# Reciprocal deviations regrouped by a small TensorE product instead of a trip through DRAM, and the third batch entry's spectrum and way back moved to later steps

## The chip, the core and the metric

One Trainium2 chip, one of its cores. The metric is the device time of one execution in microseconds (us), given as the median of several runs. Beside the runs there is one profiled execution, with a trace of every instruction; its own time and its span stand in the table below. All data are 32-bit floats.

## What is computed

The reference is a global filter over the sequence followed by a feed-forward block with a SoLU activation and a layer norm:

```python
X = np.fft.rfft(x, axis=1)                 # x: 8 entries x 3136 positions x 256 channels
Y = X * (filt_r + 1j * filt_i)[None]
x = np.fft.irfft(Y, n=3136, axis=1).reshape(25088, 256)

h = x @ w_in                               # 256 -> 1024
e = np.exp(h - max(h)); sm = e / (sum(e) + 1e-9)
solu = h * sm
ln = (solu - mean(solu)) / np.sqrt(var(solu) + 1e-6) * g_ln
out = ln @ w_out                           # 1024 -> 256
```

Maxima, sums, means and variances are taken over the 1024 features of each of the 25088 tokens. The factor 1 / sqrt(var + 1e-6) is one number per token. In the kernel it is called rs, and it is applied at the very end, when a token's output leaves PSUM.

## The kernel before, in words

**The feed-forward half** sets the rhythm. The 25088 tokens are 196 blocks of 128; two blocks make a pair, two pairs a group of four blocks (so 98 pairs and 49 groups). The program is an order written out by hand under a manual schedule: `step(k)` is called for k = 0 to 204, and each step issues work for several blocks at different ages. With j = k // 2, an even step and the odd step after it make the seven products of a 2 x 2 Strassen-like scheme for pair j (`product`, L723, on sums and differences that `pair_sums` makes on GpSimd), and the seven products of the output side for an older pair p (`project`, L844; p = j - 5 in the even step, j - 4 in the odd one). Each engine runs its own instructions in the order in which the program issues them.

Each `product` is one matmul of 128 x 512, each `project` four matmuls of 128 x 128; the trace shows every such float matmul as two weight loads and two matmul records. The results of a `project` stand in two PSUM banks, o0 and o1. ScalarE takes one out, scaled by rs (`keep_out`, L856), VectorE adds the other, scaled by rs too (`finish_out`, L860).

Between the two halves of a pair: exponential (ScalarE, L755), normalization (VectorE, L771), the sum of squares (`square`, ScalarE, L779, which leaves the variance), a transpose of 32 x 32 squares (`turn`, VectorE, L787), and the regrouping of the transposed squares by eight DMAs on SP's queue (`regroup`, L799). GpSimd then makes the sums of the output side (`project_sums`, L702).

**The deviations.** The variances of a group lie as [128 partitions, 4 blocks]. After the regrouping, the tokens stand on other partitions: row 32 b + i of a new block a holds what was row 32 a + i of old block b. So rs has to be regrouped in the same way. The kernel before does that through DRAM, once per group: in the even step, `deviations` makes rs on GpSimd (L806 and L808) and writes it by one DMA on SP's queue (L810, 2 KB); in the odd step after it, `regroup_deviations` reads it back by four DMAs on SP's queue (L816, 0.5 KB each, in pieces of one number). Only for the last group these five DMAs are on GpSimd's queue. `keep_out` and `finish_out` of the group's first pair follow some two steps later.

**The filter half** is a Fourier transform in stages, for entries 0 to 7. Entry 0 is transformed up front; each later entry is woven into the steps by the table `PLAN`, which gives three lists of steps per entry: its first stage (eight pieces), its spectrum (seven pieces) and its way back (eight pieces). For entries 2 to 7 a first-stage piece fetches a slice of x (SP's queue, L245), forms a difference on VectorE (L254) and a sum on GpSimd (`sum`, L260), multiplies late in step t (L269), and stores its result to DRAM in step t + 1 (GpSimd's queue, L280). A spectrum piece in step t fetches its part of all eight first-stage results (`fetch`, L291) and its tables (`fetch_de`, L683) on ScalarE's queue and its filter on GpSimd's queue (L642), multiplies in step t (L301), multiplies by the filter on VectorE (L322 to L324), transforms back in step t + 1 and stores in step t + 2. These fetches stand in the list `spectrum_loads[t - 2]`, which runs in the middle of step t - 2; for entry 1's pieces before step 8 and for the first piece of entry 2 they stand at the end of step t - 2 instead, in `loads`. A piece of the way back (`fetch_back` on GpSimd's queue, L356; `back_halves`, L372; `join_halves`, L385 and L386) writes 4 x 2 of the positions into `y`, from which the tokens are read. Where two pieces of the way back share a step, the second is put at the step's end.

Entry 2's spectrum stands at steps 16, 18, ..., 28 and its way back at steps 32, 34, ..., 46; its eight first-stage pieces at 5, 7, 8, ..., 13. Entry 1's way back is at steps 16 to 22.

Of the kernel before, what the change touches and what calls it, by code (L numbers as in the profile page):

```python
# [9 lines left out]
FP32 = mybir.dt.float32  # L10
I32 = mybir.dt.int32
AFT = mybir.ActivationFunctionType
ALU = mybir.AluOpType
AX = mybir.AxisListType
PSUM = bass.MemoryType.PSUM
DRAM = bass.MemoryType.DRAM

P = 128
B, S, C = 8, 3136, 256
DFF = 1024  # L20
# [16 lines left out]
PLAN = [  # L37
    None,
    ([0, 0, 0, 0, 1, 1, 1, 1], [4, 5, 6, 7, 8, 10, 12], [16, 17, 18, 19, 20, 20, 21, 22]),
    ([5, 7, 8, 9, 10, 11, 12, 13], range(16, 30, 2), range(32, 48, 2)),  # L40
    ([15, 23, 25, 27, 29, 31, 33, 35], range(38, 52, 2), range(54, 70, 2)),
    (range(39, 55, 2), range(58, 72, 2), range(76, 92, 2)),
    (range(63, 79, 2), range(82, 96, 2), range(100, 116, 2)),
# [3 lines left out]
EPS_LN, EPS_SM = 1e-6, 1e-9  # L47
# [47 lines left out]
def kernel(  # L95
# [10 lines left out]
    nc = tc.nc  # L106
# [3 lines left out]
    wi_dram = nc.inline_tensor(wi_host, name="wi_tbl").ap()  # L110
    wb_dram = nc.inline_tensor(wb_host, name="wb_tbl").ap()
    de_dram = nc.inline_tensor(de_host, name="de_tbl").ap()

    def pool(name, bufs, space=None, stack=ctx):
        kw = {} if space is None else {"space": space}
        return stack.enter_context(tc.tile_pool(name=name, bufs=bufs, **kw))
# [4 lines left out]
    small = pool("sm", 4)  # L121
# [14 lines left out]
    neg_half = consts.tile([P, 4], FP32, name="neg_half")  # L136
# [265 lines left out]
    with ExitStack() as st:  # L402
# [50 lines left out]
        second = Spectrum(1, None, None, None)  # L453
# [136 lines left out]
        for i0, n, rows in ((0, 4, P), (4, 4, P), (8, NP - 9, P), (NP - 1, 1, NQ)):  # L590
            f, at = filters[i0]
# [19 lines left out]
    def psum(name):  # L611
        return ps_t.tile([P, 2, C], FP32, name=name, tag="t")

    def psum_pair(name, other):
# [7 lines left out]
    hpool = pool("hp", 2)  # L622
    wk = pool("wk", 1)
    spool = pool("sp", 1)
    rs_dram = pool("rs_dram", 2, DRAM)
    pools |= {name: pool(name + "1", bufs)
             for name, bufs in (("r", 4), ("diff", 1), ("t2", 1), ("p", 1), ("g", 1))}
    pools["de"] = pool("de1", 2)
    second.pools = pools
    for c, at, n, kind, dims in (  # L630
            (0, 0, 4 * C, "t2", "p (v c) -> p v c"), (0, 4 * C, 4 * C, "f", "p (v k c) -> p v k c"),
# [48 lines left out]
    def load_de(sp, u):  # L680
# [3 lines left out]
                            in_=de_dram[i:i + pairs].rearrange("i p k u q -> p i (k u q)"))  # L684
        return de

    turns, variances, solu_ts, solu_sums, rs_rows, rss, pos, ots = (
        {} for _ in range(8))
    sums, ms, hs, nmaxs, es, solus, squares = {}, {}, {}, {}, {}, {}, {}


# [107 lines left out]
            nc.sync.dma_start(out=st[32 * q:32 * q + 32, :, :],  # L799
                              in_=turned[32 * a:32 * a + 32, :, q, :])  # L800

    def deviations(p, dma):
        g, second = divmod(p, 2)
        if not second:
            rs = small.tile([P, 4], FP32, name=f"rs_{g}", tag="rs", bufs=2)
            nc.gpsimd.tensor_scalar(out=rs, in0=variances.pop(g), scalar1=1.0 / DFF, scalar2=EPS_LN,  # L806
                                    op0=ALU.mult, op1=ALU.add)
            nc.gpsimd.tensor_tensor(out=rs, in0=rs, in1=neg_half, op=ALU.pow)  # L808
            rs_rows[g] = rows = rs_dram.tile([P, 4], FP32, name=f"rows_{g}", tag="rows")
            dma(out=rows, in_=rs)  # L810

    def regroup_deviations(g, dma):
        rows = rs_rows.pop(g).rearrange("(a p) b -> b p a", p=32)
        rss[g] = small.tile([P, 4], FP32, name=f"rs_t_{g}", tag="rs_t")
        for b in range(4):
            dma(out=rss[g][32 * b:32 * b + 32, :], in_=rows[b])  # L816

    def project_sums(p, step):

# [14 lines left out]
    def project(p, m):  # L834

        bank = {1: 0, 6: 0, 5: 0, 3: 0, 2: 1, 7: 1, 4: 1}[m]
        if m in (1, 2):
            pos[p, bank] = ps_o.tile([P, DFF // 2], FP32, name=f"o{m}_{p}", tag=f"o{bank}")[:, 0:P]
        s1, s2, s3, s4 = solu_sums[p]
        lhs = {1: solu_ts[p, 0][0], 2: solu_ts[p, 0][1], 4: solu_ts[p, 1][1], 5: s1, 6: s2, 7: s3,  # L840
               3: s4}[m]
        w = w_out_sb[:, {1: 0, 2: 1, 3: 2, 5: 3, 6: 4, 7: 5, 4: 6}[m]]
        for f in range(KF // 2):
            nc.tensor.matmul(out=pos[p, bank], lhsT=lhs[:, f, :], rhs=w[:, f, :],  # L844
                             start=f == 0 and m in (1, 2, 7), stop=True, skip_group_check=True)
# [32 lines left out]
    def ahead(t, by):  # L878
        return loads[max(0, t - by)]
# [3 lines left out]
    for e in range(1, B):  # L883
        first_at, spectrum_at, back_at = PLAN[e]
        sp = Spectrum(e, pools, load_filter, load_de)
        if e == 1:
            sp = second
            sp.load, sp.load_de = load_filter, load_de
        for i, t in enumerate(first_at):
            dma = nc.gpsimd.dma_start  # L890
            if e == 1:
                if i not in sp.xs:
                    row_loads.append((t, t - 1, -1, lambda sp=sp, i=i, dma=dma: sp.fetch_x(i, [dma] * 2)))
                for u in range(2):
                    (early, late)[u][t].append(lambda sp=sp, i=i, u=u: sp.first(
                        i, (u,), psum(f"pa_{sp.e}_{i}_{u}").rearrange("p a c -> p (a c)").rearrange(
                            "p (o n) -> p o n", o=1), nc.scalar.copy, sp.xs[i][0:NK, 2 * u:2 * u + 2, :]))
                    (early, late)[u][t].append(lambda sp=sp, i=i, u=u: sp.store_first(
                        i, 2 * u, nc.gpsimd.dma_start))
            else:  # L900

                row_loads.append((t, t - 2, -1, lambda sp=sp, i=i: sp.fetch_quarters(i, nc.sync.dma_start)))
                stores[t].append(lambda sp=sp, i=i: sp.difference(i))
                products[t].append(lambda sp=sp, i=i: sp.sum(i))
                late[t].append(lambda sp=sp, i=i: sp.first_quarters(
                    i, [psum(f"pa_{sp.e}_{i}_{g}") for g in range(2)]))
                stores[t + 1].append(lambda sp=sp, i=i, dma=dma: sp.store_quarters(i, dma))
        for i, t in enumerate(spectrum_at):

            other = e == 1 and i % 2 == 1 and t + 1 < LAG  # L910


            dma = nc.sync.dma_start if e == 1 and t < 8 else nc.scalar.dma_start
            fetches = ahead(t, 2) if e == 1 and t < 8 or e == 2 and i == 0 else spectrum_loads[t - 2]
            fetches.append(lambda sp=sp, i=i, dma=dma: sp.fetch(i, dma))
            ahead(t, 1 if e == 1 and i % 2 == 1 else 2).append(lambda sp=sp, i=i: sp.fetch_filter(i))
            fetches.append(lambda sp=sp, i=i: sp.fetch_de(i))
            early[t].append(lambda sp=sp, i=i, o=other: sp.forward(i, psum_pair(f"pb_{sp.e}_{i}", o)))
            add = (nc.gpsimd if t + 1 < LAG else nc.vector).tensor_tensor
            first_parts[t].append(lambda sp=sp, i=i, add=add: sp.multiply(i, 0, add))  # L920
            (top if t + 1 < LAG else second_parts)[t + 1].append(
                lambda sp=sp, i=i, add=add: sp.multiply(i, 1, add))
            late[t + 1].append(lambda sp=sp, i=i, o=other: sp.inverse(i, psum_pair(f"pc_{sp.e}_{i}", o)))
            stores[t + 2].append(lambda sp=sp, i=i: sp.store(i, nc.gpsimd.dma_start))


        assert S * (e - 1) <= P * (back_at[0] // 2 * 2) and P * (back_at[-1] + 2) <= S * e // P // 2 * 2 * P
        for ch, t in enumerate(back_at):
            row_loads.append((
                t, t - 1, spectrum_at[-1] + 2, lambda e=e, ch=ch: fetch_back(e, ch)))  # L930
            second_one = ch and t == back_at[ch - 1]
            (late if second_one else early)[t].append(lambda e=e, ch=ch: back_halves(
                e, ch, [psum(f"py_{e}_{ch}_{g}") for g in range(2)]))
            (late if second_one else middle)[t].append(lambda e=e, ch=ch: join_halves(e, ch))
# [13 lines left out]
    def step(k):  # L948
# [23 lines left out]
        if not odd:  # L972
# [25 lines left out]
            if proj:  # L998
                project(p, 3)
                keep_out(p, 0, (0, 1))  # L1000
                project(p, 4)
            for job in spectrum_loads[k]:
                job()
            if 0 <= j - 3 < pairs:
                regroup(j - 3, 0)
                regroup(j - 3, 1)
            if j - 3 == pairs - 2:
                deviations(j - 3, nc.gpsimd.dma_start)
            if 0 <= j - 4 < pairs:
                project_sums(j - 4, 1)  # L1010
            if j - 3 == pairs - 2:
                regroup_deviations((j - 3) // 2, nc.gpsimd.dma_start)
            elif 0 <= j - 3 < pairs:
                deviations(j - 3, nc.sync.dma_start)
            if hid:
                product(j, 7)
            if 2 <= k < blocks + 2:
# [6 lines left out]
        else:  # L1024
# [13 lines left out]
            if hid:  # L1038
                product(j, 3)
                product(j, 4)  # L1040
            if 0 <= j - 3 < pairs:
                if (j - 3) % 2 == 0 and j - 3 < pairs - 2:
                    regroup_deviations((j - 3) // 2, nc.sync.dma_start)
            if proj:
                project(p, 6)
                project(p, 7)
# [20 lines left out]

    with tc.manual_schedule():
        pair_sums(0)
        for load in first_loads:  # L1070
            load()
        for k in range(blocks + LAG):
            step(k)
# [30 lines left out]
```

## Time and profile before

| What | Value |
|---|---|
| Median of 3 runs | 1626.26 us (1624.71 to 1630.68) |
| The profiled execution's own time | 1619.98 us |
| Its span, first to last instruction | 1618.2 us |
| Mean granted TensorE clock | 0.991 |
| VectorE, ScalarE, GpSimd busy | 1302.4, 903.4, 1169.3 us |
| Queue q1 (the many small packets): packets, share of 16 engines | 304340, 40.3% |
| Packets under 512 B, of all 377245 | 62762 |
| L810, DMAs that write rs, on SP's queue | 48, median 552 ns to issue |
| L816, DMAs that read rs back, on SP's queue | 192, median 424 ns to issue |
| L808, the power on GpSimd | 49, mean 1034 ns |

A page of the profile gives busy time by engine, the span in 40 slices, groups of instructions by line with their mean duration and the idle time before them, and the chain of work that ended last. Engines are named PE (TensorE's matmuls), PEld (its weight loads), DVE (VectorE), ACT (ScalarE), POOL (GpSimd) and SP; an engine's name with a q, such as ACTq, is its queue that issues DMAs. In the timeline each line has start, duration, engine, line of the kernel and operation; square brackets hold the idle time before it and what ended it. A releaser is inferred from semaphores, so the name behind the arrow can be that of a bystander.

### The profile page before, as it was taken

The page shows a single profiled execution, that of the slowest core. Times are in us where ns is not written, and L with a number is a line of the kernel's source. Part 1 is how long each engine was busy: PE and PEld are TensorE (multiplying, and loading weights), DVE is VectorE, ACT ScalarE, POOL GpSimd, SP SyncE. Part 2 cuts the span into 40 slices and gives each one's busy share as a digit, 9 for nine tenths or more (in the row PEclk, how much of TensorE's full clock was granted, in tenths as well). Part 3 has the DMA queues.
Part 4 walks back from the last instruction along what each step waited for, and adds up shares of the span by engine and source line. Part 5 has one row for each costly group of instructions (what it writes and reads, how often), then busy time and mean ns, then how long its engine had stood idle before and what let it go on. Part 6 is the DMA issues. An engine that isn't in the chain of part 4 may idle for free. (4 is left out here: it accounts for less than half of the span.)

```text
span 1618.2 us, 37006 instructions
## 1 busy us (share of the span) xinstructions
PE 1548.8 (96%) x12710; PEld 1048.2 (65%) x12710; DVE 1302.4 (80%) x2630; ACT 903.4 (56%) x1772; POOL 1169.3 (72%) x1333
## 2 busy tenths in 40 slices
PE   5899899999999999999999999999999999999997
PEld 1363456666766677667766676667676777777776
DVE  1686877998898989997999789897988777777772
ACT  2135555566565655666656655566556566665662
POOL 4446887579777877797688867788666766677775
PEclk8999999999999999999999999999999999999999
DMA  9888878877788778866887668866785454444443
GB/s 268 245 268 249 244 208 229 223 209 196 203 246 231 201 189 243 241 192 167 211 251 200 186 180 229 238 180 169 215 234 151 121 135 122 104 112 105 110 110 102
DMA packets 377245, 312.13 MB, mean 193 GB/s; under 512 B 62762, under 2 KB 342835, under 8 KB 377059
## 3 DMA queue, kind: packets, MB, share of 16 engines
q1 hardware_dynamic: 304340, 168.63, 40.3%
q0 software_dynamic: 34624, 101.68, 20.7%
q10 hardware_dynamic: 38096, 39.46, 8.1%
q8 instruction: 103, 1.69, 0.5%
q14 instruction: 82, 0.67, 0.1%
HBM read 124.86 MB, written 81.50 MB: 128 GB/s over the span
## 5 line engine op out<-in xcount | busy, mean ns | idle before, releaser
L844 PEld LDWEIGHTS o<-w_out_sb,solu_t 128*128 128x128 f32 x3136 | 382.8, 192 | 49.3 <-issue 43.9
L723 PE MATMUL m<-w_in_sb,s 128*128 128x512 f32 x784 | 396.6, 607 | 9.9 <-ACT h L733 9.2
L844 PE MATMUL o<-w_out_sb,solu_t 128*128 128x128 f32 x3136 | 402.1, 276 | 2.9 <-DVE ot L860 2.0
L844 PEld LDWEIGHTS o<-w_out_sb,u 128*128 128x128 f32 x2352 | 307.3, 192 | 144.4 <-issue 109.7
L844 PE MATMUL o<-w_out_sb,u 128*128 128x128 f32 x2352 | 311.0, 275 | 7.4 <-ACT ot L856 4.6
L723 PE MATMUL m<-w_in_sb,y 128*128 128x512 f32 x588 | 308.0, 607 | 4.8 <-DVE h L744 2.9
L771 DVE SCALAR_TENSOR_TENSOR h<-e,rsum,h 128x1024 f32<-128x1024 f32 x196 | 302.1, 1541 | 6.9
L733 ACT COPY h<-m 128x512 f32<-128x512 f32 x294 | 172.9, 588 | 237.0 <-PE m L723 204.2
L702 POOL TENSOR_TENSOR u<-solu_t 128x512 f32<-128x512 f32 x98 | 133.3, 1361 | 219.3 <-DMA solu_t<-turn 134.6
L856 ACT ACTIVATE ot<-o,rs_t 128x128 f32<-128x128 f32 x392 | 143.6, 366 | 258.3 <-PE o L844 241.2
L779 ACT ACTIVATE h<-h,nmu 128x1024 f32<-128x1024 f32 x196 | 224.9, 1148 | 53.2 <-DVE turn L787 43.0
L747 DVE CUSTOM_DVE_ANT_0 h<-m,h 128x512 f32<-128x512 f32 x196 | 134.1, 684 | 140.3 <-ACT h L733 102.6
L787 DVE STREAM_TRANSPOSE turn<-h 128x1024 f32<-128x1024 f32 x196 | 243.2, 1241 | 3.2
L755 ACT ACTIVATE e<-h,nmax 128x1024 f32<-128x1024 f32 x196 | 225.1, 1149 | 8.8 <-DVE h L771 8.4
L702 POOL TENSOR_TENSOR u<-solu_t,u 128x512 f32<-128x512 f32 x98 | 149.0, 1520 | 93.4 <-PE o L844 89.2
L723 PEld LDWEIGHTS m<-w_in_sb,s 128*128 128x128 f32 x784 | 128.6, 191 | 98.3 <-issue 85.0
L860 DVE SCALAR_TENSOR_TENSOR ot<-o,rs_t,ot 128x128 f32<-128x128 f32 x294 | 102.0, 347 | 77.0 <-ACT ot L856 60.6
L723 PEld LDWEIGHTS m<-w_in_sb,y 128*128 128x128 f32 x588 | 96.3, 191 | 102.1 <-issue 52.9
L702 POOL TENSOR_TENSOR u<-u,solu_t 128x512 f32<-128x512 f32 x98 | 161.6, 1649 | 0.9
L702 POOL TENSOR_TENSOR solu_t<-solu_t,solu_t 128x512 f32<-128x512 f32 x98 | 153.4, 1565 | 7.7
L702 POOL TENSOR_TENSOR s<-y 128x128 f32<-128x128 f32 x196 | 95.6, 488 | 0.5
L372 PEld LDWEIGHTS py<-wb_t,t 50*64 50x64 f32 x3584 | 57.6, 134 | 42.9 <-issue 22.5
(116 smaller groups left out, 1965.4 us busy)
## 6 DMA issues: line engine op xcount, KB each, us to landing
solu_t<-turn SPq DMA_DIRECT2D x784, 128.0 KB
out_dram<-ot SPq DMA_DIRECT2D x196, 128.0 KB
t<-d POOLq DMA_DIRECT2D x112, 200.0 KB, 6.0
d<-x POOLq DMA_DIRECT2D x100, 200.0 KB, 5.1
f<-f_dram POOLq DMA_DIRECT2D x39, 512.0 KB, 7.2
d<-g POOLq DMA_DIRECT2D x39, 512.0 KB, 4.8
t<-d ACTq DMA_DIRECT2D x37, 512.0 KB
x<-in_x_dram SPq DMA_DIRECT2D x112, 98.0 KB
```

Source lines behind the costliest of these rows:

```text
L372: nc.tensor.matmul(out=views[g][64 * h:64 * h + 64, cb, i, :], lhsT=t4[rows, i, c0:c0 + 64], rhs=wb_t[rows, 0:N1], start=True, stop=True)
L702: nc.gpsimd.tensor_tensor(out=out, in0=in0, in1=in1, op=op)
L723: nc.tensor.matmul(out=ms[j, bank], lhsT=lhsT, rhs=w_in_sb[:, w, :], start=m in (1, 2, 7), stop=True, skip_group_check=True)
L733: nc.scalar.copy(out=h_half(k, i), in_=ms[j, 0])
L747: nc.vector.tensor_tensor_reduce(out=h_half(k, i), in0=ms[j, bank], in1=h_half(*kept), scale=1.0, scalar=sofar, op0=ALU.add, op1=ALU.min, ...
L755: nc.scalar.activation(out=e, in_=hs[k], func=AFT.Exp, bias=nmaxs.pop(k)[:, 1:2], scale=-1.0, accum_out=esum)
L771: nc.vector.scalar_tensor_tensor(out=solu, in0=e, scalar=rsum, in1=solu, op0=ALU.mult, op1=ALU.mult, accum_out=nmu)
L779: nc.scalar.activation(out=solu, in_=solu, func=AFT.Square, bias=nmu, scale=-float(DFF), accum_out=variances[g][:, i:i + 1])
L787: nc.vector.transpose(out=turns[g][:, :, i, :], in_=solus[k].rearrange("p (f j) -> p f j", j=32))
L844: nc.tensor.matmul(out=pos[p, bank], lhsT=lhs[:, f, :], rhs=w[:, f, :], start=f == 0 and m in (1, 2, 7), stop=True, skip_group_check=True)
L856: nc.scalar.activation(out=out_half(p, *to)[0], in_=pos[p, 0], func=AFT.Copy, scale=rs)
L860: nc.vector.scalar_tensor_tensor(out=ot, in0=pos[p, bank], scalar=rs, in1=out_half(p, *kept)[0], op0=ALU.mult, op1=ALU.add)
```

## The change

Two things are changed.

First, rs no longer goes through DRAM. GpSimd multiplies rs into a table of 0 and 1 (`turn_t`, first 32 columns), which gives a matrix `wide` of [128, 4 x 32] with rs on the diagonals of 32 x 32 squares. One pair's steps later, after `project(p, 4)` of the even step and so ahead of that step's `product(j, 7)`, TensorE multiplies it with the last four columns of the table (partition // 32 equals the column), and the result, [128, 4], is rs in the new order. It is written to four unused columns of the PSUM bank o1, and ScalarE copies it to SBUF. The five DMAs per group are gone, with the special path for the last group. The table, 128 x 36, is fetched once at the start on GpSimd's queue.

Second, entry 2's spectrum moves from steps 16 ... 28 to 18 ... 30. Its way back moves from 32, 34, ..., 46 to 34, 36, ..., 46, 46, so that the last two pieces share step 46. The fetches of its first spectrum piece now stand in the middle of a step, as those of the others.

```diff
-    ([5, 7, 8, 9, 10, 11, 12, 13], range(16, 30, 2), range(32, 48, 2)),
+    ([5, 7, 8, 9, 10, 11, 12, 13], range(18, 32, 2), [34, 36, 38, 40, 42, 44, 46, 46]),
...
+    rows = np.arange(P)[:, None]
+    turn_dram = nc.inline_tensor(np.concatenate(
+        [rows % 32 == np.arange(32), rows // 32 == np.arange(4)], 1).astype(np.float32),
+        name="turn_tbl").ap()
...
-    rs_dram = pool("rs_dram", 2, DRAM)
...
+    spread = pool("spread", 1)
+    turn_t = spread.tile([P, 36], FP32, name="turn_t", tag="turn_t")
...
-    def deviations(p, dma):
-        g, second = divmod(p, 2)
-        if not second:
-            rs = small.tile([P, 4], FP32, name=f"rs_{g}", tag="rs", bufs=2)
-            nc.gpsimd.tensor_scalar(out=rs, in0=variances.pop(g), scalar1=1.0 / DFF, scalar2=EPS_LN,
-                                    op0=ALU.mult, op1=ALU.add)
-            nc.gpsimd.tensor_tensor(out=rs, in0=rs, in1=neg_half, op=ALU.pow)
-            rs_rows[g] = rows = rs_dram.tile([P, 4], FP32, name=f"rows_{g}", tag="rows")
-            dma(out=rows, in_=rs)
-
-    def regroup_deviations(g, dma):
-        rows = rs_rows.pop(g).rearrange("(a p) b -> b p a", p=32)
+    def deviations(g):
+        rs = small.tile([P, 4], FP32, name=f"rs_{g}", tag="rs", bufs=2)
+        nc.gpsimd.tensor_scalar(out=rs, in0=variances.pop(g), scalar1=1.0 / DFF, scalar2=EPS_LN,
+                                op0=ALU.mult, op1=ALU.add)
+        nc.gpsimd.tensor_tensor(out=rs, in0=rs, in1=neg_half, op=ALU.pow)
+        spreads[g] = wide = spread.tile([P, 4, 32], FP32, name=f"wide_{g}", tag="wide")
+        nc.gpsimd.tensor_tensor(
+            out=wide, in0=turn_t[:, 0:32].rearrange("p (o i) -> p o i", o=1).broadcast_to([P, 4, 32]),
+            in1=rs.rearrange("p (b o) -> p b o", o=1).broadcast_to([P, 4, 32]), op=ALU.mult)
+
+    def regroup_deviations(g, ps):
+
+        nc.tensor.matmul(out=ps, lhsT=spreads.pop(g).rearrange("p b i -> p (b i)"), rhs=turn_t[:, 32:36],
+                         start=True, stop=True)
         rss[g] = small.tile([P, 4], FP32, name=f"rs_t_{g}", tag="rs_t")
-        for b in range(4):
-            dma(out=rss[g][32 * b:32 * b + 32, :], in_=rows[b])
+        nc.scalar.copy(out=rss[g], in_=ps)
...
-            pos[p, bank] = ps_o.tile([P, DFF // 2], FP32, name=f"o{m}_{p}", tag=f"o{bank}")[:, 0:P]
+            ps = ps_o.tile([P, DFF // 2], FP32, name=f"o{m}_{p}", tag=f"o{bank}")
+            pos[p, bank] = ps[:, 0:P]
+            places[p] = ps[:, P:P + 4]
...
-            fetches = ahead(t, 2) if e == 1 and t < 8 or e == 2 and i == 0 else spectrum_loads[t - 2]
+            fetches = ahead(t, 2) if e == 1 and t < 8 else spectrum_loads[t - 2]
...
                 project(p, 4)
+            if j >= 4 and j % 2 == 0 and j - 4 < pairs:
+                regroup_deviations((j - 4) // 2, places.pop(p) if proj else psum("ps_rs")[:, 0, 0:4])
...
-            if j - 3 == pairs - 2:
-                deviations(j - 3, nc.gpsimd.dma_start)
             if 0 <= j - 4 < pairs:
                 project_sums(j - 4, 1)
-            if j - 3 == pairs - 2:
-                regroup_deviations((j - 3) // 2, nc.gpsimd.dma_start)
-            elif 0 <= j - 3 < pairs:
-                deviations(j - 3, nc.sync.dma_start)
+            if 0 <= j - 3 < pairs and j % 2:
+                deviations((j - 3) // 2)
...
-            if 0 <= j - 3 < pairs:
-                if (j - 3) % 2 == 0 and j - 3 < pairs - 2:
-                    regroup_deviations((j - 3) // 2, nc.sync.dma_start)
...
         pair_sums(0)
+        nc.gpsimd.dma_start(out=turn_t, in_=turn_dram)
```

More of the change, by code (lines that the diff above doesn't have):

```diff
@@ L685, in load_de @@
         return de
-    turns, variances, solu_ts, solu_sums, rs_rows, rss, pos, ots = (
-        {} for _ in range(8))
+    turns, variances, solu_ts, solu_sums, spreads, rss, pos, ots, places = (
+        {} for _ in range(9))
     sums, ms, hs, nmaxs, es, solus, squares = {}, {}, {}, {}, {}, {}, {}
```

## The prediction, made before the result was known

> **What bounds the kernel now.** I read the page's head first, then busy time by stretches of the span.
>
> ```profile
> span 1618.2 us, 37006 instructions
> PE 1548.8 (96%) x12710; PEld 1048.2 (65%) x12710; DVE 1302.4 (80%) x2630; ACT 903.4 (56%) x1772; POOL 1169.3 (72%) x1333
> PE   5899899999999999999999999999999999999997
> ```
>
> ```profile
> 120.00:250.00 130.00, 113.96 (x612) 59.89 (x612) 96.98 (x186) 67.58 (x128) 100.48 (x122) 0.97 0.82 238
> 250.00:400.00 150.00, 146.01 (x1471) 99.35 (x1470) 130.37 (x257) 87.07 (x173) 110.18 (x131) 1.00 0.77 211
> 400.00:880.00 480.00, 476.06 (x4399) 326.69 (x4399) 428.88 (x839) 285.95 (x567) 369.92 (x424) 1.00 0.78 216
> 880.00:1060.00 180.00, 177.19 (x1585) 120.41 (x1584) 151.60 (x306) 107.24 (x213) 138.00 (x160) 1.00 0.72 204
> 1060.00:1565.00 505.00, 504.70 (x3906) 360.97 (x3906) 406.77 (x878) 305.74 (x606) 365.91 (x402) 1.00 0.54 143
> ```
>
> The first pair of numbers is the stretch's length and PE's busy time. From 250 us to 1565 us PE idles 11 us in all. There only less PE work, or one of few stalls, can shorten the kernel, and PE work added is paid in full. Between 120 and 250 us it idles 16 us, the largest stall being this, in the timeline of ACT and then of PE:
>
> ```profile
> 237.89 0.37 ACT L856 ACTIVATE ot<-o,rs_t 128x128 f32<-128x128 f32 x1
> 243.67 0.38 ACTq L291 DMA_DIRECT2D t<-d  x1
> 244.08 0.57 ACTq L683 DMA_DIRECT2D de<-de_tbl  x1
> 244.70 0.58 ACT L733 COPY h<-m 128x512 f32<-128x512 f32 x1 [6.44 <-issue]
> ```
>
> ```profile
> 245.43 2.04 PE L723 MATMUL m<-w_in_sb,s 128*128 128x512 f32 x2 [3.36 <-ACT h L733]
> ```
>
> Entry 2's first spectrum fetch stands at the end of step 14 on ACT's queue and waits until all first-stage stores have landed; GpSimd issued the last of them at 238.80 to 239.83. `keep` (L733) is queued behind it, and PE's third product behind that. Then PE ran slow (two matmuls in 2.04 us where 1.02 is usual), about 1.8 us more until 250 us: 5.1 us together.
>
> **What the Trainium skill says.** "TensorE: Matmul & The Clock Gate", section "LDWEIGHTS (loading the stationary operand)": a load takes its number of columns / 1.2 ns, so 107 ns for 128 columns, whatever the moving operand. The trace agrees: the way back of entry 0 moves only 98 columns, yet its 128 loads ran back to back, 14.5 / 128 = 113 ns apart, about as far as those of `project`, which move 128 columns (16 records in 1.78 us by the chain of waits: 111 ns).
>
> ```profile
> L395 PEld LDWEIGHTS py<-wi_t,t 100*128 100x128 f32 x128 | 14.5, 192 | 0.5 <-issue 0.5
> L702 POOL TENSOR_TENSOR s<-y 128x128 f32<-128x128 f32 x196 | 95.6, 488 | 0.5
> ```
>
> The same page, "Part 2: What happens when you issue a matmul", says that loads are pulled ahead of running matmuls into a background buffer. In `project` load and matmul take alike, so no slack hides another load. "DMA: Bandwidth & Descriptors", "Anatomy of one DMA — SWDGE (gpsimd) path", puts the fixed cost of a DMA near 2 us, mostly the write's receipt; the five DMAs pay it twice. In the trace GpSimd's pair for the last group took 2.2 and 3.8 us to land.
>
> **The change, part by part.**
>
> *Added on PE.* 49 products of a 128-column weight with 4 columns, two records each as for every float matmul. No row shows four moving columns. Low bound: the loads hide, and two records cost what the closest-spaced ones of the trace do (the way back's L372, 64 in 0.97 us, 15 ns): 0.03 us. High bound: both loads are exposed with their whole 192 ns, and the records come on top: 0.41 us. I take two load paces, 2 x 0.111 = 0.222 us, because the product sits between a stream that is as fast as its loads and the first load of `product(j, 7)`. Groups 0 and 48 fall in idle time; 47 x 0.222 = **+10.4 us** (1.4 to 19.3).
>
> *Added on GpSimd.* One multiply of 128x128 per group, like the row of 488 ns: 24 us in all, and one 0.55 us DMA issue at the start, beneath the 28% of the span that GpSimd idles. Broadcast operands are not shown; below nothing is excluded, since it is extra work. GpSimd waits over 300 us in the run, mostly for solu_t. Queued behind the multiply are filter fetches, stores and the sum L260, for which PE's first-stage product waits. In step 10 PE idles 0.97 us for that sum: **+0.5 us**. Were GpSimd's slack gone in five early groups, 2.5 us.
>
> *Added on ACT.* 49 copies of four columns, at most the 0.37 us of the 128-column row. ACT waits there for PE: behind `keep_out` it queues `g` and `t` copies, spectrum fetches and `keep` of product 5, which PE makes only after 4, the small product and 7. So nothing; VectorE's `finish_out` may wait on the bank for some 0.3 us, under GpSimd's and PE's distance of over 2 us.
>
> *Removed from SP's queue.* 48 x 0.552 + 192 x 0.424 = 108 us of issuing, and waits between (31.2 us for the row to land). SP is not PE's limit in general, but in one place the read-back came late:
>
> ```profile
> 1044.23 0.58 ACT L733 COPY h<-m 128x512 f32<-128x512 f32 x1 [2.25 <-DMA de<-de_tbl]
> 1049.05 0.37 ACT L856 ACTIVATE ot<-o,rs_t 128x128 f32<-128x128 f32 x1 [4.24 <-DMA rs_t<-rows]
> ```
>
> PE then idled 1.02 us: **-1.0**. Earlier solu_t and x between 160 and 400 us: **-1.0**, an estimate (0 to -4: the stalls there that name POOL sums or rows). At the end, GpSimd's write (0.29 + 0.66 us) stood ahead of the u for which PE waited 1.33 us; the 0.49 us multiply replaces it: **-0.4**.
>
> *Moved: entry 2's fetches.* At step 16 the stores of step 14 have landed, so ACT's wait goes. What is late next is GpSimd's sum of entry 3's first piece, in GpSimd's timeline:
>
> ```profile
> 242.90 0.19 POOL L806 TENSOR_SCALAR rs<-var 128x4 f32<-128x4 f32 x1
> 243.17 1.04 POOL L808 TENSOR_TENSOR rs<-rs,neg_half 128x4 f32<-128x4 f32 x1
> 244.18 0.83 POOL L642 DMA_DIRECT2D f<-f_dram  x1
> 245.01 2.07 POOL L356 DMA_DIRECT2D t<-d  x4
> 247.10 1.28 POOL L260 TENSOR_TENSOR x<-x 113x512 f32<-113x512 f32 x1
> ```
>
> PE's product on it began at 250.76 and would be reached 5.1 us earlier, at 245.7. The sum ends at 248.38; the filter fetch leaves (-0.83, it moves two steps with its piece), the multiply comes (+0.49): 248.04. That alone gains 2.6 us. GpSimd had waited 3.81 us for solu_t, whose DMAs SP issued from 222.28, after 3.10 us of read-back; the transpose was done at 218.9. So up to 5.1 us. I take **-3.5**.
>
> *Moved: the rest.* Seven spectrum pieces leave step pair 16 and enter pair 30, with two ACT issues, a filter and a store on GpSimd's queue each; the total is unchanged. Where entry 1's way back and entry 2's spectrum meet, PE idled 0.62, 0.96 and 0.62 us for VectorE; the first of these goes (-0.6). The way back's fetches (GpSimd, 0.54 us each), PE's 64 records (0.97 us), ACT's copy (0.49) and VectorE's two joins (1.11) go two steps later; step 46 has them twice. Entry 1 has the same double at step 20, where PE idled 0.39 us (+0.4). The tokens are first summed in step 47, and multiplied in 48. Together **-0.2**.
>
> Sum: 10.4 + 0.5 - 1.0 - 1.0 - 0.4 - 3.5 - 0.2 = **+4.8 us**. The span goes from 1618.2 to 1623.0, the profiled execution from 1619.98 to 1624.8. That execution lies 6.3 us below the median of the runs, so for the metric I add the difference: 1626.26 + 4.8 = **1631.1 us**.
>
> **The rivals.**
>
> *A, the loads hide* (faster). For it: PEld is busy 65% and loads are pulled ahead. Against: the 113 ns row. With 1.4 instead of 10.4, the full 5.1 instead of 3.5, and 3 us instead of 1 from SP: 4.8 - 9.0 - 1.6 - 2 = -7.8, **1618.5**.
>
> *B, an exposed turnaround* (slower). Mechanism: at the seam between `project(p, 4)` and `product(j, 7)`, the short product empties PE's pipeline. Price 0.41 us x 47 = 19.3 instead of 10.4: 4.8 + 8.9 = +13.7, **1640.0**. From 0.222 + 3.3 / 47 = 0.29 us apiece it decides. For it: nothing as short is in the trace, and the weights wait for GpSimd's semaphore. Against: the existing seams cost nothing (14 products at the pace of 12.25 us per pair).
>
> *C, the moved fetch does nothing* (within, at the edge): the ACT wait gives way to the sum and to entry 3's own such wait (PE idle 2.36 us at 489 us, untouched). Gain 0.5 instead of 3.5: **1634.1**.
>
> **How the numbers follow.** About 0.5%, 8.1 us, is what a measurement of this kernel can tell from no change. Forecast 0.45 (1627 to 1635), A 0.20 (1614 to 1624), B 0.20 (1634.4 to 1646), C 0.15 (1631 to 1637). Faster: nearly half of A, 0.09, and 0.01 elsewhere. Slower: nearly all of B, half of C, a little of the forecast: 0.30. The range, 1618 to 1641, leaves out A's lower edge and B's upper half.
>
> **What would show it.** The small product's records with 0.22 us between the neighbours; PE's busy time up by about 10 us and its idle time down by 6; no ACT gap over 5 us at step 14; PE's wait for L260 there 2 us or so; nobody waiting for rs_t. I am wrong if the pair's pace of 12.25 us after 1400 us is unchanged in steps with the product, or lengthened by over 0.3 us.

## The result, and the profile after

The kernel after takes **1614.79 us**, median of six runs (1611.29 to 1617.59), against 1625.49 us of the kernel before beside it (six runs, 1623.17 to 1633.11): a ratio of 0.9913 [0.9885, 0.9940]. A second comparison gave 1615.20 against 1628.01 us, 0.9918 [0.9885, 0.9951]. So it is faster by 11 to 13 us, where +4.8 us were forecast, and it lies below the range. The profiled execution took 1613.7 us. From the head of its page and from busy time by stretches (length, then PE's busy time, then PEld, DVE, ACT and POOL):

```profile
span 1611.8 us, 36836 instructions
PE 1553.6 (96%) x12808; PEld 1058.6 (66%) x12808; DVE 1309.3 (81%) x2630; ACT 911.3 (57%) x1821; POOL 1194.2 (74%) x1378
```

```profile
120.00:250.00 130.00, 117.64 (x644) 61.64 (x642) 102.94 (x190) 72.29 (x137) 104.29 (x126) 0.97 0.82 241
250.00:400.00 150.00, 147.74 (x1478) 101.76 (x1479) 131.04 (x262) 88.45 (x179) 113.57 (x136) 1.00 0.78 221
400.00:880.00 480.00, 479.11 (x4431) 330.49 (x4430) 430.60 (x839) 287.46 (x580) 381.21 (x443) 1.00 0.77 215
880.00:1060.00 180.00, 180.00 (x1619) 124.67 (x1618) 158.85 (x317) 108.86 (x221) 141.93 (x169) 1.00 0.73 207
1060.00:1565.00 505.00, 504.80 (x3921) 363.02 (x3920) 400.98 (x866) 306.80 (x621) 372.55 (x415) 1.00 0.52 141
```

PE is busier by 4.8 us in the whole span, and it idles 11.2 us less, so the span is 6.4 us shorter. Between 120 and 250 us PE idles 12.4 us (16.0 before), between 250 and 1565 us 3.3 us (11.0 before). From 400 to 1565 us hardly a stall is left: 1.1 us of 1165.

**The small product** can be read in the chain of work that ended last, at one even step (start, duration, engine, tile, line, records):

```profile
1001.68 1.78 PE o L852 x16
1003.47 0.12 PE o L819 x2
1003.59 1.82 PE m L728 x4
1005.41 1.78 PE o L852 x16
1007.20 1.72 PE m L728 x4
```

It takes 0.12 us, and the next product takes 1.82 us, where one without it takes 1.72: **0.22 us**, the forecast price to the digit. After 1250 us, where PE never waits in either kernel, the lead of the kernel after shrinks from 7.8 us (step 145) to 5.1 (step 195): 2.7 us over 12 small products, 0.22 each.

**Step 14.** In the timelines of GpSimd and PE, where before ACT held everything up for 6.44 us:

```profile
241.70 0.40 POOL L813 TENSOR_TENSOR wide<-turn_t,rs 128x128 f32<-128x128 f32 x1
242.26 2.15 POOL L360 DMA_DIRECT2D t<-d  x4 [0.16 <-issue]
244.43 1.28 POOL L264 TENSOR_TENSOR x<-x 113x512 f32<-113x512 f32 x1
```

```profile
245.76 0.72 PE L273 MATMUL pa<-x,wq_t 49*64 49x512 f32 x2 [1.38 <-POOL x L264]
```

ACT's gap is gone, and GpSimd's sum is late next: PE waits 1.38 us for it. The multiply with its two broadcast operands takes 0.40 us.

**SP's queue** is where the forecast had looked least. The waits of SP's own queue, 250 to 1060 us, before and then after (line, what ended the wait; us in total, times, longest):

```profile
SPq L799 <- DVE turn L787: 42.7, 14, 8.9
SPq L799 <- PE o L844: 34.3, 32, 3.0
SPq L799 <- DMA t<-d: 28.0, 7, 7.4
```

```profile
SPq L804 <- PE o L819: 118.3, 25, 10.3
SPq L804 <- DVE turn L792: 80.1, 24, 6.6
```

These lines are `regroup`. When SP waits there for the transpose (turn), or for PE to give a buffer free, it has arrived ahead of its data or of its buffer. All lines of `regroup` that name PE or VectorE together make 94 us before and 229 us after. Nearly all the rest of its waits name other DMAs, as the third line does: 72 us before and 32 after. So before, SP had less than half of this lead; it came later to data that stood ready, and the products' inputs came later with it.

### The profile page after: what moved, and what is told of

Its sections match the earlier page's. It is cut to its first block, busy times and chain, and to the rows that moved or that the text cites. A ratio compares the mean times of both kernels' runs of the same rounds, so it can differ in the third digit from the quotient of the medians.

```text
span 1611.8 us, 36836 instructions
## 1 busy us (share of the span) xinstructions
PE 1553.6 (96%) x12808; PEld 1058.6 (66%) x12808; DVE 1309.3 (81%) x2630; ACT 911.3 (57%) x1821; POOL 1194.2 (74%) x1378
## 3 DMA queue, kind: packets, MB, share of 16 engines
q1 hardware_dynamic: 269780, 168.42, 39.6%
## 4 chain that ended last, share of the span: by engine, by line
PE 68%; DMA 1%; DVE 1%; issue 0%; ACT 0%; SPq 0%; POOL 0%; POOLq 0%; DVEq 0%; ACTq 0%
PE o L852 30%; PE m L728 29%; PE py L376 3%; PE pc L305 2%; PE pa L273 2%; PE pb L305 2%; DMA solu_t<-turn 0%; DMA out_dram<-ot 0%; PE o L819 0%; DVE h L776 0%; SPq L804 0%; ACT e L760 0%; DVE h L752 0%; ACT ot L864 0%; DVE h L749 0%
## 5 line engine op out<-in xcount | busy, mean ns | idle before, releaser
L776 DVE SCALAR_TENSOR_TENSOR h<-e,rsum,h 128x1024 f32<-128x1024 f32 x196 | 313.4, 1599 | 6.9
L707 POOL TENSOR_TENSOR u<-u,solu_t 128x512 f32<-128x512 f32 x98 | 167.4, 1709 | 0.9
L707 POOL TENSOR_TENSOR s<-y 128x128 f32<-128x128 f32 x196 | 99.0, 505 | 0.7 <-ACT y L402 0.3
```

Of the source, the lines that this page charges most:

```text
L707: nc.gpsimd.tensor_tensor(out=out, in0=in0, in1=in1, op=op)
L776: nc.vector.scalar_tensor_tensor(out=solu, in0=e, scalar=rsum, in1=solu, op0=ALU.mult, op1=ALU.mult, accum_out=nmu)
```

## The experiments

The theory after the result (T1): the product costs 0.22 us a group, and the trip through DRAM, not the plan, was worth well over the 2.4 us that the forecast gave it. Rivals: the gain is only that nobody waits late for rs_t, wherever its DMAs stand (T2); the moved plan brings it (T3); the small product is cheaper than it looks (T4); the change of buffers does it (T5, formed on the way). The first three are Theory 1 to 3 of the expectations. The runs were made on five chips; the kernel before, run beside these kernels on each, had medians of 1626.6 to 1628.0 us.

**The two halves apart.** `product_only` is the kernel after with the old plan and the old place of the first fetch; `plan_only` is the kernel before with the new ones.

`product_only`, against the kernel after:

```diff
-    ([5, 7, 8, 9, 10, 11, 12, 13], range(18, 32, 2), [34, 36, 38, 40, 42, 44, 46, 46]),
+    ([5, 7, 8, 9, 10, 11, 12, 13], range(16, 30, 2), range(32, 48, 2)),
...
-            fetches = ahead(t, 2) if e == 1 and t < 8 else spectrum_loads[t - 2]
+            fetches = ahead(t, 2) if e == 1 and t < 8 or e == 2 and i == 0 else spectrum_loads[t - 2]
```

> The kernel after with entry 2's plan and its first fetch put back as they were before: only the small product is new. Theory 1 (the trip through DRAM cost far more than the small product, because its five DMAs per group stood on SP's queue ahead of solu_t and x): 4 to 9 us faster than before, with the ACT wait of over 5 us in step 14 still there. Theory 2 (what was gained is that nobody waits late for rs_t; the queue doesn't matter): also faster than before, 2 to 8 us. Theory 3 (entry 2's later spectrum brought nearly all, and the product's 10 us are lost): 3 to 10 us slower than before.

> The kernel before with entry 2's spectrum and way back at the later steps and its first fetch in the middle of a step; rs still goes through DRAM. Theories 1 and 2: 3 to 6 us faster than before, the ACT wait in step 14 gone, PE then waiting 1 to 3 us for GpSimd's sum. Theory 3: 12 to 20 us faster than before, and faster than the kernel after.

`product_only`: 1617.63 us, 0.9940 [0.9920, 0.9960], so 9.8 us less. `plan_only`: 1627.53 us, 1.0000 [0.9983, 1.0017], nothing, where all three theories had expected a gain. T3 falls. In the trace of `plan_only` the wait at step 14 is gone and 7 us are won by step 25, but they, and as much again, are lost between steps 27 and 117, in stalls of 0.9 to 2.3 us behind GpSimd, ScalarE and VectorE. With the product, the plan seems worth 2.4 to 2.8 us by the medians, but the intervals overlap (0.9913 and 0.9918 against 0.9940). In `product_only` the fetch still stands at its old place, but at step 14 PE waits only 0.50 us for ScalarE, where it had waited 3.36 before:

```profile
240.81 1.10 PE L728 MATMUL m<-w_in_sb,s 128*128 128x512 f32 x2 [0.50 <-ACT h L738]
```

If the product costs 10.4 us and the whole brings -9.8, taking the trip away is worth about -20 us.

**The price of the product**, made twice in every group:

```diff
-        nc.tensor.matmul(out=ps, lhsT=spreads.pop(g).rearrange("p b i -> p (b i)"), rhs=turn_t[:, 32:36],
-                         start=True, stop=True)
+        wide = spreads.pop(g).rearrange("p b i -> p (b i)")
+        for _ in range(2):
+            nc.tensor.matmul(out=ps, lhsT=wide, rhs=turn_t[:, 32:36], start=True, stop=True)
```

> The kernel after with the small product made twice, one after the other, into the same four columns (the second overwrites the first with the same numbers). If a product costs two load paces, as forecast: 47 x 0.222 = 10.4 us slower than the kernel after (9 to 12). If the loads hide: within 2 us of it.

1627.46 us, 1.0004 [0.9981, 1.0028]: 12 to 13 us above the kernel after, 0.25 to 0.26 for each of 49 further products. T4 falls: the product is paid in full.

**The trip put back** beside the product. rs goes to DRAM in `deviations` and comes back in the odd step as before, into a tile that nothing reads, so the output is unaffected (in this kernel and in all others with a tile `back`).

```diff
+        nc.sync.dma_start(out=rows, in_=rs)
...
+        back = small.tile([P, 4], FP32, name=f"back_{g}", tag="back")
+        for b in range(4):
+            nc.sync.dma_start(out=back[32 * b:32 * b + 32, :], in_=rows[b])
```

> The kernel after, and beside the small product the five DMAs per group are issued on SP's queue where they were before, into a tile that nobody reads; only the last group goes without. The output doesn't depend on them. Theory 1 (place on the queue and in the DMA engines): 8 to 16 us slower than the kernel after, so about as slow as before or slower. Theory 2 (late numbers): within 3 us of the kernel after, since nobody waits for the tile. Theory 3: within 3 us too.

1652.25 us, 1.0151 [1.0120, 1.0183]: 37 us above the kernel after, more than twice the 8 to 16 us that T1 had expected. Two variants, one with pieces of 16 bytes (another order of the numbers in `back`) and one with the reads a step later, were as slow (1654.40 and 1653.48 us, four runs each):

> As trip_added_back, but the four DMAs read rows of 16 bytes (32 pieces each in place of 128 pieces of 4 bytes; the order of the numbers is then wrong, and nobody reads them). Theory packets (the 512 small pieces per group burden the DMA engines): 1615 to 1628 us. Theory head of line (SP stands until the row has landed, solu_t and x behind it) and theory issue (SP's 1.7 us of issuing): as trip_added_back, 1643 to 1655 us.

> As trip_added_back, but the four DMAs (4-byte pieces as before) are issued a step later, ahead of the next even step's solu_t, when the row has long landed, so SP doesn't stand for it. Theory head of line: 1615 to 1630 us. Theory packets and theory issue: 1643 to 1655 us.

All three carried a second change: `back` made the pool `small` grow by 64 bytes per partition, and so moved every pool behind it. Two kernels measured that by itself: the kernel after with an unused tile of 64 bytes, or of 512 (then [P, 32] in place of [P, 4]).

```diff
+    pad = small.tile([P, 4], FP32, name="pad", tag="pad")
+    nc.vector.memset(pad, 0.0)
```

> The kernel after with one unused tile of four buffers of 16 bytes per partition added to the pool of small tiles, and one memset at the start: nothing else is done, but every pool that is opened later lies 64 bytes further on in SBUF. The three kernels that read a tile back have exactly this shift, and all took about 1653 us, whatever they read and when; the one that only writes has not, and took 1615. Theory place in SBUF: 1640 to 1656 us. Theory DMAs: as the kernel after, 1611 to 1618 us.

> As pad_64_bytes, but the unused tile takes 4 x 128 bytes per partition, so the later pools lie 512 bytes further on. If the 16 us of pad_64_bytes come from where the pools lie within 512 bytes: as the kernel after, 1611 to 1619 us. If an extra tile or any shift costs: 1625 to 1635 us.

64 bytes: 1630.41 us, 1.0026 [1.0008, 1.0043], 15 to 16 us above the kernel after. 512 bytes: 1615.81 us, 0.9924 [0.9894, 0.9954], nothing. So neither the extra tile nor a shift as such costs, but the place within 512 bytes, or within a part of them, does. The queue lines (packets, MB, share of 16 engines) of the kernel after and of the kernel with 64 bytes show the same packets taking longer (with 512 bytes they took 39.5%):

```profile
q1 hardware_dynamic: 269780, 168.42, 39.6%
```

```profile
q1 hardware_dynamic: 269780, 168.42, 42.7%
```

The Trainium skill, "DMA: Bandwidth & Descriptors", section "How a descriptor splits into AXI transactions", says that when a descriptor (one contiguous piece of a DMA) does not start at a multiple of 256 bytes, its first transaction starts at the 256-byte boundary below, and that the unused bytes are paid. The measurement agrees: 42.7 against 39.6% of a longer span is 9% more packet time with 64 bytes, and none more with 512. T5 can't explain the kernel after, though, whose new pool stands behind all others.

With `back` in that last pool, nothing else moves:

> As trip_added_back, but the tile that the four DMAs fill lies in the last pool of SBUF, so that nothing else is moved. Theory place in SBUF: the 38 us of trip_added_back shrink to what the trip itself costs, which the runs so far put at up to 20 us: 1615 to 1636 us. Theory DMAs: 1645 to 1657 us.

1631.35 us, 1.0020 [0.9997, 1.0043]: the trip alone costs **16 to 17 us**. That is T1 by direct measurement, and T2 falls, since nobody waits for `back`. Only the write of it (48 DMAs) costs nothing:

> As trip_added_back (which took 1652 us, some 37 us more than the kernel after), but only the write of rs is issued, 48 DMAs on SP's queue; nothing is read back. If SP's standing still for the row to land is the cost, or the 4-byte pieces, or the four issues: within 6 us of the kernel after (1612 to 1621). If the write's own wait for GpSimd's power is the cost (SP stands until rs is there, with solu_t and x queued behind): 15 us or more slower than the kernel after.

1614.73 us, 0.9919 [0.9889, 0.9949].

**How the trip costs.** The trace of `trip_back_at_the_end` can be laid beside that of the kernel after. VectorE's last transpose of a pair and SP's queue, in the kernel with the trip, and then in the kernel after:

```profile
449.68 1.25 DVE L793 STREAM_TRANSPOSE turn<-h 128x1024 f32<-128x1024 f32 x1
```

```profile
447.93 3.07 SPq L249 DMA_DIRECT2D x<-in_x_dram  x4
451.10 3.63 SPq L830 DMA_DIRECT2D back<-rows  x4
454.82 10.81 SPq L805 DMA_DIRECT2D solu_t<-turn  x8
```

```profile
442.44 1.25 DVE L792 STREAM_TRANSPOSE turn<-h 128x1024 f32<-128x1024 f32 x1
```

```profile
438.67 12.03 SPq L804 DMA_DIRECT2D solu_t<-turn  x8
```

With the trip, SP has issued the last of the eight regrouping DMAs at 465.63, 14.7 us after the transpose; without it at 450.70, 7.0 us after. The line of the four reads takes 3.63 us, and the queue had come to it late already. GpSimd's next sum then waits for solu_t, with the trip and without:

```profile
471.78 1.28 POOL L708 TENSOR_TENSOR u<-solu_t 128x512 f32<-128x512 f32 x1 [8.79 <-DMA solu_t<-turn]
```

```profile
458.97 1.28 POOL L707 TENSOR_TENSOR u<-solu_t 128x512 f32<-128x512 f32 x1 [4.39 <-DMA solu_t<-turn]
```

and behind it, on GpSimd's queue, stands the sum for the next entry's first stage, which PE then lacks:

```profile
484.56 1.12 PE L273 MATMUL pa<-x,wq_t 49*64 49x512 f32 x2 [2.51 <-POOL x L264]
```

The kernel after has no PE stall over 0.88 us past 250 us.

The loss is not spread but comes in a few places. Measured at VectorE's maxima, the kernel with the trip is 10.8 us behind in step 1 already, before its first trip, and still 9 to 11 us from step 15 to 43. Then the distance grows to 13 or 14 us (steps 51 to 65), 17 (69 to 85), 18 to 19 (87 to 113) and 23 at step 121, where it stays to the end. So 12 to 14 us are the trip's in this pair of profiles; the rest is the start of an execution that took 1637.21 us, 6 above its kernel's median. The distance grows where one entry's spectrum runs beside the next one's first stage (steps 39 to 50, 63 to 70, 87 to 94 and 111 to 118 in `PLAN`), where ScalarE's and SP's queues have fetches of both. SP is ahead of PE and VectorE for 85 us between 250 and 1060 us, as in the kernel before (94), against 229 in the kernel after.

**What SP waits for.** The line of the four reads is mostly waiting. Its issues take 0.41, 0.42, 0.30 and 0.30 us; between them SP stood twice until stores of the output had landed, and one of the regrouping DMAs behind them stood 2.7 us until an earlier one had. From SP's waits between 447 and 466 us:

```profile
SPq L805 <- DMA solu_t<-turn: 2.7, 1, 2.7
SPq L830 <- DMA out_dram<-ot: 2.1, 2, 1.2
```

The semaphores in the traces tell why. A DMA raises its semaphore when it lands. In these programs the DMAs of SP's and of ScalarE's queue take turns on the same eight semaphores (1622 DMAs before, 203 or 202 on each; 1382 after, 173 or 172 on each), and in the traces each was issued only after the one before it on its semaphore had landed in full. So a read takes one turn of eight, however small it is. For landings of other DMAs, `regroup` waited 76 us with the trip between 250 and 1060 us, against 72 in the kernel before and 32 in the kernel after. No run changes the number of semaphores, so it is argued and not shown that the reads cost their time in this way.

**Which part of the reads.** Three kernels read back one step later, all with `back` in the last pool: with four DMAs as before; with four DMAs in pieces of 16 bytes; and with one DMA of 128 pieces of 16 bytes.

```diff
 late_one_at_the_end, in place of the four:
+        nc.sync.dma_start(out=back, in_=rows)
```

> As trip_back_at_the_end (1631 us), but the four DMAs are issued a step later, when the row has landed. Theory head of line (SP stands for the row's landing, with x and solu_t queued behind): 1612 to 1621 us. Theory pieces and theory issue: 1625 to 1636 us.

> As late_at_the_end, and the four DMAs read 32 pieces of 16 bytes each in place of 128 of 4 bytes (the numbers in another order, read by nobody). Theory pieces: 1612 to 1621 us. Theory issue: 1625 to 1636 us. Theory head of line: as late_at_the_end.

> As late_compact_at_the_end, but one DMA reads all 128 pieces of 16 bytes, so that SP issues one in place of four. Theory issue (SP's time, 4 x 0.42 us per group): 1612 to 1622 us. If a read-back costs by being there at all, whatever its form: 1625 to 1636 us.

1630.68 us (1.0015 [0.9991, 1.0038]), 1634.17 (1.0032 [1.0005, 1.0058]) and **1615.98** (0.9922 [0.9894, 0.9951]). Waiting for the row to land is not it, and the small pieces are not it: one DMA is free, four cost 15 to 19 us. With one, SP is ahead for 156 us between 250 and 1060 us, and `regroup` waits 47 us for landings. The Trainium skill, "DMA: Bandwidth & Descriptors", section "Rules for kernel authors", advises to join many small transfers into one; this is a case where joining four transfers of 0.5 KB is worth 1% of a kernel. That one DMA doesn't yield the order which the kernel needs; a single read in that order wasn't tried.

**The reads on ScalarE's queue.** If only SP's queue were the limit, the kernel with the new plan, no product and its four reads issued from ScalarE should beat all others:

```diff
-                regroup_deviations((j - 4) // 2, places.pop(p) if proj else psum("ps_rs")[:, 0, 0:4])
+                regroup_deviations((j - 4) // 2, nc.scalar.dma_start)
```

> rs goes through DRAM as before (no small product, no multiply into the table), with the later plan; SP writes the row, and the four read-backs are issued on ScalarE's queue in the next even step, at the place where the kernel after has its product. If SP's issues were the cost, this keeps the gain and doesn't pay the product's 10 us: 1603 to 1610 us. If ScalarE's 4 x 0.35 us per group or the late landing of rs_t delay the output side: 1613 to 1630 us.

> As reads_on_act, with the plan of before (entry 2's spectrum from step 16, its first fetch at the end of step 14). If the later plan is worth what the forecast said (3.7 us): 3 to 6 us slower than reads_on_act. If it is worth nothing, as in plan_only: within 2 us of it.

1648.12 us, 1.0123 [1.0083, 1.0162], and 1650.47 with the old plan, 1.0141 [1.0101, 1.0180]: a clear miss, slower than either expectation. SP is ahead for 159 us there, as hoped, but ScalarE pays. The wait of its copies out of PSUM in the whole run, and its timeline at the worst place:

```profile
ACT h L733 <- DMA rs_t<-rows: 83.5, 25, 7.0
```

```profile
448.01 4.82 ACTq L816 DMA_DIRECT2D rs_t<-rows  x4
453.09 0.38 ACTq L291 DMA_DIRECT2D t<-d  x1
454.20 0.38 ACTq L683 DMA_DIRECT2D de<-de_tbl  x1
454.63 0.59 ACT L733 COPY h<-m 128x512 f32<-128x512 f32 x1 [7.01 <-DMA rs_t<-rows]
```

`keep` (L733) stands behind the four reads on ScalarE's queue, and PE then waited 3.62 us for it. Of the 4.82 us of the reads only 1.64 are issuing; the rest is waiting until DMAs of SP's queue have landed, since both queues share the eight semaphores. The two queues have 1627 DMAs here, about as many as before, and `regroup` waited 115 us for landings. So the reads are still in SP's way, and on ScalarE's queue their waiting also stands directly between PE and its consumer. What the trip's removal would bring without the product on PE was not seen.

**A cheaper product.** rs split into two bfloat16 parts (their sum replaces rs, so its last bits differ) and multiplied by two single-record products:

```diff
+        nc.gpsimd.tensor_copy(out=parts[:, 0:4], in_=rs)
+        nc.gpsimd.tensor_tensor(out=parts[:, 4:8], in0=rs, in1=parts[:, 0:4], op=ALU.subtract)
...
+        for n in range(2):
+            nc.tensor.matmul(out=ps, lhsT=wide[:, P * n:P * n + P], rhs=turn_b[:, 32:36],
+                             start=n == 0, stop=n == 1)
```

> The kernel after with the small product in bfloat16: rs is split into a bfloat16 number and the bfloat16 rest, GpSimd multiplies both into the table (one more copy, one more subtraction of four columns and twice the multiply), and TensorE makes two products of one record each in place of one product of two records. rs is kept to about 16 bits. If a product's cost is its weight load at the pace of the 32-bit stream (0.111 us a record), nothing changes: 1612 to 1618 us. If bfloat16 weights load faster, 0.05 to 0.15 us less per group: 3 to 7 us faster than the kernel after.

1614.99 us, 0.9925 [0.9896, 0.9955]: as the kernel after. On PE the price falls to 0.14 us, but GpSimd's multiply grows to 0.62 us and has two more operations before it, and PE idles 4.4 us between 400 and 880 us where the kernel after idles 0.9. No version here beats the kernel after.

**The kernel before once more**, to see how typical its profile was, and the kernel after once more:

> The kernel before, unchanged, for a second profile: the first one lay 6 us below the median of the runs. If the first was a lucky execution, this one shows more PE idle time between 250 and 1565 us than its 11 us, in stalls that lead back to SP's queue (solu_t, x or rs_t late), 14 to 25 us; if the profile is typical, 9 to 13 us.

> The kernel after, unchanged, for the comparison on one chip: 1612 to 1618 us.

The second profile of the kernel before took 1632.63 us (one run), span 1630.8. Two of its stretches, to be laid beside those shown with the prediction:

```profile
400.00:880.00 480.00, 473.67 (x4367) 324.16 (x4366) 416.65 (x826) 282.63 (x562) 362.59 (x421) 0.99 0.78 213
880.00:1060.00 180.00, 172.11 (x1542) 117.75 (x1540) 149.19 (x300) 101.08 (x201) 132.44 (x155) 1.00 0.73 200
```

From 250 to 1565 us PE idled 20.1 us here, against 11.0 in the first profile, mostly in other places: 2.94 us at 490 us behind ScalarE (2.36 in the first), 2.17 at 682 behind GpSimd, and four stalls of 1.0 to 3.9 between 1000 and 1058 behind VectorE and ScalarE. That they lead back to SP's queue, as expected, was not traced. In the second profile of the kernel after PE idled 3.1 us in this stretch, against 3.3 in the first. In that last comparison eleven runs of the kernel before spread from 1616.9 to 1636.3 us, six of the kernel after from 1612.9 to 1617.8. So the stalls of the kernel before move from run to run.

## Why the prediction was wrong, point by point

- **Added on PE, +10.4: right.** 0.22 us in the chain, 0.22 from the pace, 0.25 to 0.26 from the doubled product. That it is two weight loads is the forecast's account; no run varies the weight's columns. The sign in the sums did not come out: busy time rose by 4.8 us and not by 10, idle time fell by 11.2 and not by 6; where the other busy time went was not traced. Rival A, whose number (1618.5) came nearest, was wrong in its mechanism, so that it came near by luck: the loads do not hide. Rival B's turnaround of 0.29 us and more didn't appear.
- **Added on GpSimd, +0.5, and on ACT, 0: small, as forecast.** The multiply took 0.40 instead of 0.488 us, ScalarE's copy of four columns 0.16 us. The +0.5 had the wrong sign: PE's wait of 0.97 us in step 10, which was to grow, is gone (its product begins at 214.25 us without a gap). The trace of before names the row's write there, but the sum L260 that PE needed ended only at 215.35 us; in the kernel after it ended at 214.04, and GpSimd's sums ahead of it, which had waited 4.44 us for their input before, had not waited. Nobody waits long for rs_t: VectorE 8.6 us in 23 waits, off PE's path.
- **Moved, entry 2's fetches, -3.5: right in the trace, nothing by itself in the time.** ACT's gap went, and GpSimd's sum was late next, as forecast. But in `plan_only` what was won came back as later stalls, so rival C was nearer for this term. And in `product_only` most of this stall went without the move. A stall that goes is a gain only if the queues that follow have slack. The small rest of the plan (-0.2) can't be told apart.
- **Removed from SP's queue, -1.0 -1.0 -0.4 = -2.4: this step failed.** The trip was worth 16 to 17 us by putting it back and about 20 by `product_only`. The forecast had the 108 us of issuing in hand and priced it by a few stalls of one profile: one beneath the name rs_t, one at the end, and an estimate for 160 to 400 us. Most of its cost bears another name: SP came late to `regroup`, so solu_t was late for GpSimd, and its sums were late for PE. "SP is not PE's limit in general" was the wrong sentence. The estimate (0 to -4) also looked in the wrong place: in the pair of profiles above, the kernel with the trip loses its 12 to 14 us after step 43, that is after 400 us.
- **The sum's base.** The profile of before lay 6.3 us below the median, and the forecast carried these 6.3 us over as a constant. By the second profile they look like stalls of the kind that the change removes: it idles 9 us more than the first.

With -17 to -20 in place of -2.4, the forecast's own sum gives -10 to -13 us; measured were -10.7 and -12.8. Only the 17 tests the sum, for the 20 was itself taken from a measured total. What stays open is how three further reads a group, 48 times, become 15 to 19 us: the turns on the eight semaphores are a candidate, at one place the path to PE is shown above, and for the other places only the growth where two entries overlap speaks.

## What to carry to other kernels

Before you price what leaves a DMA queue, read that queue's own waits: if it waits little for the engines that make its data, and much for other DMAs to land, it runs late, and each DMA taken from it can be worth more than the stalls that bear its tile's name. Then count DMAs, not bytes: here one read instead of four was as good as none, and the same four on another queue with the same semaphores were no help. A stall seen in one execution of a kernel whose runs spread over 19 us is a sample of its stalls, not their list.

## What was not expected of the hardware

- Moving SBUF pools by 64 bytes costs 15 to 16 us (1630.41 against about 1615), by 512 bytes nothing (1615.81), with the same packets.
- A write of 2 KB to DRAM and its wait per group cost nothing (1614.73 us), and with one read of 128 pieces of 16 bytes neither (1615.98); with four reads of the same bytes the trip costs 15 to 19 us.
- A product of a 128-column weight with four columns costs 0.22 us in the float stream and 0.14 us as two bfloat16 products.
- DMAs of SP's and ScalarE's queues waited for each other's landings in these traces, through the eight semaphores that they share.
